# The prologue of an attention, rational and Sinkhorn-MoE kernel: load order, first two chunks of w_in, and the layout of q and k

## The chip, the cores and the metric

The kernel runs as one program on one core of a Trainium2 chip. The metric is the device time of one execution in microseconds (us). The core's engines are TensorE (PE in the profile, with its weight loads as PEld), VectorE (DVE), ScalarE (ACT), GpSimd (POOL) and SyncE (SP), which here only issues DMAs.

## The reference

Three layers follow each other; every layer feeds the next. The inputs q, k and v have 4 batches, 8 heads, 576 positions and 64 values a head; x then has 2304 rows of 512.

```python
scores = q @ k.T / sqrt(64)
mask_plain = (rel >= 0) & (rel < 32)                   # heads 0 to 3
mask_dil = (rel >= 0) & (rel < 128) & (rel % 4 == 0)   # heads 4 to 7
x = softmax(where(mask, scores, -1e9)) @ v             # to (2304, 512)

h = x @ w_in                                           # (512, 2048)
g = (a0 + a1*h + a2*h**2 + a3*h**3) / (1 + |b0|*|h| + |b1|*h**2 + 1e-6)
x = g @ w_out                                          # (2048, 512)

P = exp(x @ w_gate - max); 8 rounds of row and column scaling
out = sum over 8 experts of P[:, e] * (relu(x @ w1[e]) @ w2[e])
```

w_in and w_out arrive as 64-bit floats, and the kernel makes 32-bit floats of them itself.

## The kernel before

**Prologue.** The attention of batch 0 runs alone (`att_pieces(0)`, 52 pieces, then `flush`). Heads go in pairs (`pr` 0 and 1 are plain heads, 2 and 3 dilated ones), and each pair in three groups `jj` of 192 queries. A pair has four `prep` pieces (transposes of q and k on PE, evacuated to `qT` and `kT` by the ACTIVATE of L355), a group has a `qk` piece (scores, L363 and L370; maximum on DVE, L388; three Exp on ACT, L390; scaling on POOL, L396), a `tr` piece (transposes of the probabilities, L405, evacuated in L410) and an `av` piece (the product with v, L429, then a split into two float16 parts by L229 on ACT and L232 on DVE). The split needs a power of two for all of v's first half: `v_load` brings that half in three loads of 768 KB, `v_scan` takes its absolute maximum (L484), `v_scale` makes the scale (L207, L180, L194, L222 to L226). `coef0` (L557 to L560) prepares the rational function's coefficients from `abt`.

**Weights.** w_in is handled in four chunks of 512 columns. `wi_load(c)` issues four loads of 512 KB (L166). `wi_conv(c, kk)` turns a fourth of a chunk into float32 by `to_f32` (a Prelu on ACT, L492, and two operations on DVE, L496 and L497) and takes its maximum on ACT (L526). `wi_scale(c)` makes the chunk's scale and coefficients (L567). `wi_split(c, kk)` writes two float16 parts (L229 on ACT, L232 on DVE, 128x512). w_out is handled in sixteen blocks `f` by `wo_load` and `wo_split` (the same `to_f32`, then L607 on ACT and L611 on POOL).

**Rational stage.** 96 steps (six token blocks of 384 times sixteen blocks `f` of 128 columns) run as a pipeline: `rat_l1` (L634 to L636, twelve matmuls), the polynomials on ACT, DVE and POOL, and five steps later `rat_l2` (L694 to L696). Step `f` of the first block needs chunk `f // 4` of w_in, and block `f` of w_out five steps later. Each step has four slots in which other work is emitted: the attention of batches 1 to 3 (steps 0 to 14, 15 to 38, 43 to 62), the rest of w_in, w_out, and the maximum of v's second half. After it comes the MoE stage, almost all of the remaining time, with its own hand-placed slots.

**What sets the order.** The list of calls gives each instruction a place in an order of priority; a planner then simulates the program with costs of its own and orders each engine's instructions, so that a lower one can be taken ahead when the planner expects a higher one to wait. Attention pieces get a higher priority. What it has ordered is executed in order on each engine. `tc.add_manual_dep` adds a real wait of one instruction for another. `load` makes a DMA wait for the instruction in `gate_mm`: during the prologue the first matmul of the last emitted `qk`, later that of the last emitted `rat_l1`; while `gate_mm` is empty it waits for nothing. All loads are issued on SP's queue, in one order.

In the kernel before, the prologue's loads go out as: pair 0, v for two groups, pair 1, `abt`, v's first half, pair 2, v for six groups, pair 3. `extra` gives what is emitted after a piece of the prologue: `wi_load(0)` after piece 12, `wi_load(1)` after piece 30, `wi_conv(0, kk)` after 30, 32, 34 and 36, `wi_scale(0)` after 47, `wi_split(0, kk)` after 48 to 51. Chunk 1 is converted and split in slots of the rational stage's steps 0 to 3, though the planner took its conversion ahead.

For the plain heads, `att_load` puts positions 96c to 96c+95 into 96 partitions, for c = 0 to 5. A transposed third of a half is then a run of neighbouring positions:

```python
w, n = (QB, 6) if pr < 2 else (72, 8)
rows = [[D, w], [w * D, n], [1, D]] if pr < 2 else [[n * D, w], [D, n], [1, D]]
```

Of the kernel before, what the change touches and what calls it, by code (L numbers as in the profile page):

```python
# [10 lines left out]
F32 = mybir.dt.float32  # L11
# [16 lines left out]
def kernel(  # L28
# [14 lines left out]
    nc = tc.nc  # L43
# [152 lines left out]
    def across_sum(out_, in_, n):  # L196
        bt = side_matmul("smps", n, one.to_broadcast([P, P]), in_)
        nc.vector.tensor_scalar(out=out_, in0=bt[:, 0:n], scalar1=1e-9, scalar2=None, op0=ALU.add)

    def delayed(fn, k):  # L200
        return fn() if k == 0 else lambda: delayed(fn, k - 1)

# [64 lines left out]
    def att_load(b, pr, stage=None):  # L267
        off = (b * H + 2 * pr) * HSTR
        st = att.setdefault((b, pr), {})
        if stage:  # L270
            both = room(stage, [P, 2, 1024], F32)
        w, n = (QB, 6) if pr < 2 else (72, 8)
        rows = [[D, w], [w * D, n], [1, D]] if pr < 2 else [[n * D, w], [D, n], [1, D]]
        for i, (src, tag) in enumerate(((q, "aq"), (k, "ak"))):
            if stage:
                t = both[:w, i, 0:2 * n * D].rearrange("p (c h d) -> p h c d", c=n, h=2)
            else:
                t = room(tag, [w, n, 2, D], F32).rearrange("p c h d -> p h c d")
            for h in range(2):
                nc.sync.dma_start(out=t[:, h], in_=bass.AP(src.tensor, off + h * HSTR, rows))  # L280
            st[tag] = t.rearrange("p h c d -> p c (h d)")
# [49 lines left out]
    def att_prep(b, pr, x):  # L331
        st = att[b, pr]
        which, y = divmod(x, 2)
        key = "ak" if which else "aq"
        src = st[key]
        alt = b < 1 and pr % 2
        if x == 0:
            if ("qkT", alt) not in att:
                att["qkT", alt] = att_qk_tiles(alt)
            st["qT"], st["kT"] = att["qkT", alt]  # L340
        d = st["kT"][:, 32:] if which else st["qT"]
        if y == 1:
            st.pop(key)
        w, n = (QB, 3) if pr < 2 else (72, 4)
        bt = bank("qkps")
        for c in range(n):
            nc.tensor.transpose(bt[:, c * w:(c + 1) * w], src[:, n * y + c, :], ident[:w, :w])

        def after():
            if pr < 2:  # L350
                dv, ps = d[:, y * HS:(y + 1) * HS], bt[:, 0:HS]
            else:
                dv = d.rearrange("m (c p y) -> m y c p", c=4, y=2)[:, y]
                ps = bt[:, 0:HS].rearrange("m (c p) -> m c p", c=4)
            nc.scalar.activation(dv, ps, AF.Copy, scale=1.0 if which else QSCALE)  # L355

        return after

    def att_qk(b, pr, jj):
        st = att[b, pr]  # L360
        bt = bank("scps")
        i0 = MASK_AT[pr // 2, jj]
        mm = nc.tensor.matmul(bt[:, 0:3 * KW], ident_b, masks[:, i0:i0 + 3, :].rearrange("p a b -> p (a b)"), start=True, stop=False)  # L363
        if b == 0:
            gate_mm[0] = mm.ins
        for i in range(3):
            j = 3 * jj + i
            for h in range(2):
                hd = slice(h * D, (h + 1) * D)
                nc.tensor.matmul(  # L370
                    bt[hd, i * KW:(i + 1) * KW],
                    st["qT"][hd, j * 64:(j + 1) * 64],
                    st["kT"][hd, j * 64:j * 64 + KW],
                    start=False,
                    stop=i == 2,
                )
        sc = bt[:, 0:3 * KW].rearrange("q (i c) -> q i c", i=3)
        i = b * NG + pr * 3 + jj
        sx = sb.tile([P, 4, 3], F32, tag="asx", bufs=4, name="sx")
        y = i % (6 if b < 2 else 2)  # L380
        if y < 2:
            p = sb.tile([P, 3, KW], F32, tag=f"ap{y}", name="p")
        else:
            p = xpair[0][:, 3 * KW * (y - 2):3 * KW * (y - 1)].rearrange("p (a b) -> p a b", a=3)
        st["p", jj] = p

        def after():
            nc.vector.tensor_reduce(out=sx[:, 0, :], in_=sc, axis=AX, op=ALU.max, negate=True)  # L388
            for i in range(3):
                nc.scalar.activation(p[:, i, :], sc[:, i, :], AF.Exp, bias=sx[:, 0, i:i + 1], accum_out=sx[:, 1, i:i + 1])  # L390
            return norm

        def norm():
            nc.vector.tensor_scalar(out=sx[:, 2, :], in0=sx[:, 1, :], scalar1=1e-9, scalar2=None, op0=ALU.add)
            nc.vector.reciprocal(out=sx[:, 3, :], in_=sx[:, 2, :])
            nc.gpsimd.tensor_tensor(out=p, in0=p, in1=sx[:, 3, :].unsqueeze(2).to_broadcast([P, 3, KW]), op=ALU.mult)  # L396

        return after
# [81 lines left out]
    def v_scan(hf, i):  # L480
        t = vst.pop((hf, i))
        m = vmx[:, 6 * hf + 2 * i:6 * hf + 2 * i + 2]
        for j in range(2):
            nc.vector.tensor_reduce(out=m[:, j:j + 1], in_=t[:, j * NV // 2:(j + 1) * NV // 2], axis=AX, op=ALU.max, apply_absolute_value=True)  # L484

    def v_scale(hf):
        return pow2_scale(vmx[:, 6 * hf:6 * hf + 6], 6, 14, s_x1[:, hf:hf + 1], i_x1[:, hf:hf + 1], lag=hf)

    def to_f32(src, y, dst):
        w = src.rearrange("p (n two) -> p n two", two=2)  # L490
        lo, hi = w[:, :, 0], w[:, :, 1]
        nc.scalar.activation(y, hi.bitcast(F32), AF.Prelu, scale=float(2.0**-112), alpha=-float(2.0**32))  # L492
        d = y.bitcast(I32)

        def bits():
            nc.vector.tensor_scalar(out=d, in0=d, scalar1=3, scalar2=None, op0=ALU.logical_shift_left)  # L496
            nc.vector.scalar_tensor_tensor(out=dst.bitcast(I32), in0=lo, scalar=29, in1=d, op0=ALU.logical_shift_right, op1=ALU.bitwise_or)  # L497

        return bits
# [21 lines left out]
    def wi_conv(c, kk):  # L521
        x = wx[c][:, kk, :]
        i = c * KD + kk

        def mx():
            nc.scalar.activation(junk, x, AF.Abs, accum_out=wmx[:, i:i + 1])  # L526

        if not wide:
            junk = room(WI_ST[c][kk // 2], [P, 512], F32)
            return mx  # L530
        st = wst.pop((c, kk))
        junk = st[:, 0:512].bitcast(F32)
        bits = to_f32(st, x, x)

        def then():
            bits()
            return mx

        return then
# [50 lines left out]
    def wo_split(f):  # L590
# [4 lines left out]
        hi, lo = wo_hi[c][:, g, :], wo_lo[c][:, g, :]  # L595
        x, y = wst.pop(("o", f))
        if wide:
            bits = to_f32(x, y, y)
            x = y

        def s1():
# [10 lines left out]

        return s1


    behind = {}

    def pin(eng, i):
        if eng in behind:
            tc.add_manual_dep(i.ins, behind[eng], mybir.DependencyInfo(mybir.DependencyClass.Sync, mybir.DependencyReason.DATA), reason="behind work that others wait for")  # L620

    cur = {}
    SEQ = [(n, f, f == 0, f == NF1 - 1) for n in range(NB) for f in range(NF1)]
# [1 line left out]
    def rat_l1(st, half):  # L625
# [6 lines left out]
        for kk in (2 * half, 2 * half + 1):  # L632
# [3 lines left out]
            nc.tensor.matmul(hp, wlo, xb[:, 0, kk, :], start=False, stop=kk == KD - 1)  # L636
            if kk == 0:
                gate_mm[0] = mm.ins

    def cf(st):  # L640
        n, f, _, _ = SEQ[st]
# [494 lines left out]

    LAG = 5
    ATT = ((1, 0, 14), (2, 15, 38), (3, 43, 62))
    WO = [f if f < 8 else 11.75 + (f - 8) // 2 * 1.5 + 0.5 * (f % 2) for f in range(NF1)]
    WI_S = (None, 0, 4, 7.5)  # L1140

    def att_pieces(b):
        groups = [(pr, jj) for pr in range(H // 2) for jj in range(3)]
# [141 lines left out]
            if callable(more):  # L1285
                at(s + 1, more)

    for c in range(1, 4):
        s = int(4 * WI_S[c])
        for kk in range(KD):  # L1290
            at(s + 1 + 2 * kk, wi_conv, c, kk)
            at(s + (12 if c > 1 else 11) + kk, wi_split, c, kk)
        at(s + 10, wi_scale, c)
    for c in (2, 3):
        at(int(4 * WI_S[c]) - (6 if c == 2 else 4), wi_load, c)
    at(4 * 20, lambda: load(wgr, w_gate.rearrange("(k p) e -> p k e", p=P)))
    at(4 * 26 + 1, wg_prep)
    for i in range(3):
        at(4 * 1 + 8 * i, v_load, 1, i, "x2_4")
        at(4 * (1 + 2) + 8 * i, v_scan, 1, i)  # L1300
    at(4 * (1 + 8), v_scale, 1)
    at(4 * 13, coefs, 1, 0, 4)


    att_load(0, 0)
    for i in range(2):
        att_load_v(i)
    att_load(0, 1, "R1")
    nc.sync.dma_start(out=abt[:, 0:4], in_=ra.partition_broadcast(P))
    nc.sync.dma_start(out=abt[:, 4:6], in_=rb.partition_broadcast(P))  # L1310
    for i in range(3):
        v_load(0, i, f"x2_{3 + i}")
    att_load(0, 2, "R2")
    for i in range(2, 4):
        att_load_v(i)
    for i in range(4, 8):
        att_load_v(i)
    att_load(0, 3, "R3")
    pcs = att_pieces(0)
    extra = defaultdict(list)  # L1320
    extra[12].append(lambda: wi_load(0))
    extra[30].append(lambda: wi_load(1))
    av0 = next(i for i, pc in enumerate(pcs) if pc[0] == "av")
    extra[av0 - 1] += [lambda i=i: v_scan(0, i) for i in range(3)] + [lambda: v_scale(0), coef0]
    n = len(pcs)
    for kk in range(KD):
        extra[30 + 2 * kk].append(lambda kk=kk: wi_conv(0, kk))
        extra[n - 4 + kk].append(lambda kk=kk: wi_split(0, kk))
    extra[n - 4 - 1].append(lambda: wi_scale(0))
    for f in range(2):  # L1330
        extra[44 + f].append(lambda f=f: wo_load(f))
    later = []
# [89 lines left out]
```

## Time and profile before

| what | value |
|---|---|
| median of 3 runs | 1957.07 us (1953.51 to 1958.82) |
| time of the profiled execution | 1955.98 us |
| its span, first to last instruction | 1954.0 us |
| busy share of the span: PE, DVE, ACT, POOL | 96%, 79%, 62%, 25% |
| mean granted TensorE clock | 0.981 of full speed |

The profiled execution lies 1.1 us under the median, and 2.0 us of it lie outside the span. A row of instructions in the profile has a start, a length, the engine, the source line, the operation, output and inputs by name (`roomA`, `roomV` and `roomIG` are large shared buffers); a bracket at its end says how long the engine had been idle before it and what ended that. "SPq" rows are DMA issues in SP's queue.

### The profile page before, as it was taken

The numbers are of one execution on the slowest core, as the hardware profiler recorded it, in microseconds if no ns is written. First come the engines' busy times: TensorE is split into PE (matmuls) and PEld (weight loads), VectorE is DVE, ScalarE is ACT, GpSimd is POOL, SyncE is SP. The second block draws the span as 40 slices with busy tenths as digits, with TensorE's granted clock in tenths as the row PEclk, the third lists the DMA queues.
The fourth block names the chain that finished last, engine by engine and source line by source line (L and its number), as shares of the span: only waits on it lengthen the run. The fifth ranks groups of instructions, "written<-read, shape, count | busy, mean of one in ns | idle before, by whom it ended". The sixth has DMA issues, their size and how long they took to land. (4 is left out here: it accounts for less than half of the span.)

```text
span 1954.0 us, 36520 instructions
## 1 busy us (share of the span) xinstructions
PE 1875.1 (96%) x14202; PEld 1410.8 (72%) x14202; DVE 1543.8 (79%) x2516; ACT 1217.3 (62%) x2182; POOL 493.2 (25%) x489
## 2 busy tenths in 40 slices
PE   6688999999999899999999999999999999999998
PEld 5466777777776677777777777777777777777776
DVE  4799769678998999778688778877878787786754
ACT  5788777777776545647556655664656566465652
POOL 1233422222232023015113211411421231141110
PEclk6789999999999999999999999999999999999999
DMA  6744113122212351564454357345435534633323
GB/s 172 214 135 125 32 38 104 34 59 76 92 38 80 124 157 68 190 185 128 94 141 125 56 120 184 69 109 143 103 62 135 155 74 112 165 87 78 86 54 53
DMA packets 208269, 207.92 MB, mean 106 GB/s; under 512 B 78176, under 2 KB 155488, under 8 KB 208096
## 3 DMA queue, kind: packets, MB, share of 16 engines
q1 hardware_dynamic: 191232, 173.09, 29.4%
q0 software_dynamic: 16864, 32.51, 11.2%
q8 instruction: 111, 1.82, 0.4%
q14 instruction: 62, 0.51, 0.1%
HBM read 155.86 MB, written 49.68 MB: 105 GB/s over the span
## 5 line engine op out<-in xcount | busy, mean ns | idle before, releaser
L922 PEld LDWEIGHTS <-roomA 128*128 128x128 f16 x3276 | 318.9, 98 | 182.1 <-issue 14.2
L922 PE MATMUL l1a<-roomA 128*128 128x384 f16 x1872 | 355.8, 326 | 3.3 <-ACT roomV L971 2.5
L922 PE MATMUL l1b<-roomA 128*128 128x384 f16 x1404 | 273.6, 326 | 5.4 <-DVE roomA L973 3.4
L680 POOL TENSOR_TENSOR roomIG<-roomA,roomIG 128x384 fp32r<-128x384 f32 x96 | 118.2, 1242 | 230.6 <-ACT roomIG L679 206.0
L944 POOL TENSOR_TENSOR roomIG<-roomA 128x384 f32<-128x384 f32 x48 | 60.2, 1254 | 456.8 <-ACT roomA L978 344.3
L1022 PE MATMUL yps<-roomA 128*128 128x256 f16 x630 | 169.9, 273 | 2.4 <-DVE roomV L1048 1.5
L1022 PE MATMUL yps<-roomA,roomV 128*128 128x256 f16 x630 | 168.9, 273 | 3.1 <-DVE roomA L1045 3.1
L1023 PE MATMUL yps<-roomA,roomV 128*128 128x256 f16 x630 | 170.5, 273 | 0.8 <-DVE roomA L885 0.8
L1023 PE MATMUL yps<-roomA 128*128 128x256 f16 x630 | 170.9, 273 | 0.0
L1024 PE MATMUL yps<-roomA,roomV 128*128 128x256 f16 x630 | 169.4, 273 | 0.0
L1024 PE MATMUL yps<-roomA 128*128 128x256 f16 x630 | 169.1, 273 | 0.0
L871 POOL TENSOR_TENSOR roomA<-roomA 128x256 f32<-128x256 f32 x140 | 133.2, 971 | 35.0 <-DVE roomA L885 23.1
L695 PE MATMUL o1ps<-roomIG,roomV 128*128 128x384 f32 x384 | 137.0, 357 | 1.5 <-POOL roomIG L680 1.2
L885 DVE SCALAR_TENSOR_TENSOR roomA<-roomA,sm 128x768 f16<-128x768 f32 (+1 forms) x92 | 112.2, 1232 | 25.1 <-ACT roomA L882 24.3
L634 PE MATMUL h1ps<-roomA 128*128 128x384 f16 x384 | 128.5, 335 | 2.7 <-DVE roomA L660 1.3
L696 PE MATMUL o1ps<-roomIG,roomV 128*128 128x384 f32 x384 | 130.0, 341 | 0.0
L636 PE MATMUL h1ps<-roomA 128*128 128x384 f16 x384 | 127.9, 333 | 0.2 <-DVE roomA L232 0.2
L635 PE MATMUL h1ps<-roomA 128*128 128x384 f16 x384 | 128.0, 333 | 0.0
L944 POOL TENSOR_TENSOR roomIG<-roomV 128x384 f32<-128x384 f32 x48 | 51.1, 1064 | 288.7 <-ACT roomV L978 246.7
L1022 PEld LDWEIGHTS <-roomA 128*128 128x128 f16 x1008 | 98.4, 98 | 28.7 <-DVE roomA L1048 3.4
L1023 PEld LDWEIGHTS <-roomV 128*128 128x128 f16 x1008 | 98.4, 98 | 27.4 <-issue 4.2
L882 ACT ACTIVATE roomA<-roomA,sm 128x768 f16<-128x768 f32 (+1 forms) x92 | 93.9, 1036 | 38.9 <-POOL roomA L871 17.0
(221 smaller groups left out, 4925.5 us busy)
## 6 DMA issues: line engine op xcount, KB each, us to landing
roomA<-xd SPq DMA_DIRECT2D x119, 384.0 KB
roomA<-in_moe_w_dram SPq DMA_DIRECT2D x240, 128.0 KB
roomA<-in_moe_w_dram SPq DMA_DIRECT2D x120, 256.0 KB
out_dram<-roomV POOLq DMA_DIRECT2D x31, 512.0 KB, 5.7
out_dram<-roomA POOLq DMA_DIRECT2D x31, 512.0 KB, 5.8
roomV<-in_moe_w_in_dram SPq DMA_DIRECT2D x16, 512.0 KB
roomA<-in_moe_w_out_dram SPq DMA_DIRECT2D x16, 512.0 KB
xd<-roomA SPq DMA_DIRECT2D x14, 384.0 KB
```

The lines of the kernel that those rows point to most:

```text
L634: mm = nc.tensor.matmul(hp, whi, xb[:, 0, kk, :], start=kk == 0, stop=False)
L635: nc.tensor.matmul(hp, whi, xb[:, 1, kk, :], start=False, stop=False)
L636: nc.tensor.matmul(hp, wlo, xb[:, 0, kk, :], start=False, stop=kk == KD - 1)
L680: nc.gpsimd.tensor_tensor(out=gl, in0=g, in1=gh.bitcast(F32), op=ALU.subtract)
L695: nc.tensor.matmul(ob[dd], hi, d["gl"], start=False, stop=False)
L696: nc.tensor.matmul(ob[dd], lo, d["gh"], start=False, stop=last)
L871: pin("p" if pool else "v", eng.tensor_tensor(out=d[:, o, :], in0=a, in1=b, op=ALU.add if w == 0 and n == 0 else ALU.subtract))
L885: pin("v", nc.vector.scalar_tensor_tensor(out=l, in0=x, scalar=sc, in1=h, op0=ALU.mult, op1=ALU.subtract))
L922: mm = nc.tensor.matmul(ps, w[:, wx_, wh, kk * P:(kk + 1) * P], x[:, xh, kk, :], start=start and kk == 0 and wh == 0 and xh == 0, stop=sto ...
L1022: nc.tensor.matmul(o, hh[:, a - 1, c], w[:, m, 0, :], start=i == 0 and half == 0, stop=False)
L1023: nc.tensor.matmul(o, hh[:, a - 1, c], w[:, m, 1, :], start=False, stop=False)
L1024: nc.tensor.matmul(o, hl[:, a - 1, c], w[:, m, 0, :], start=False, stop=i == NP - 1 and (last or half == 1 or b == 3))
```

## The change

q and k of the plain heads are loaded with six neighbouring positions to a partition, as the dilated heads have eight; the evacuation in L355 then writes every sixth element of `qT` or `kT`. Pair 2 and v's scan are loaded ahead of `abt`, `wi_load(0)` is issued at the start, between `abt` and pair 3, and waits for nothing. `wi_load(1)` moves from piece 30 to 20. Both chunks are converted, scaled and split inside the prologue. A Prelu of `to_f32` now waits: for the last emitted Exp in chunks 0 and 1 ("x"), for the first matmul of the last emitted `rat_l1` in chunks 2 and 3 and in w_out ("m"); so do the maxima of v's second half. Chunk 2 moves two steps ahead (4 to 2), chunk 3 one and a half (7.5 to 6), the second half of v five steps later, and w_out's blocks 8 to 15 come once a step from step 10.25 (before: two in 1.5 steps from 11.75).

```diff
-        rows = [[D, w], [w * D, n], [1, D]] if pr < 2 else [[n * D, w], [D, n], [1, D]]
+        rows = [[n * D, w], [D, n], [1, D]]
...
             if pr < 2:
-                dv, ps = d[:, y * HS:(y + 1) * HS], bt[:, 0:HS]
+                dv = d.rearrange("m (p c) -> m c p", c=2 * n)[:, n * y:n * (y + 1)]
             else:
                 dv = d.rearrange("m (c p y) -> m y c p", c=4, y=2)[:, y]
-                ps = bt[:, 0:HS].rearrange("m (c p) -> m c p", c=4)
+            ps = bt[:, 0:HS].rearrange("m (c p) -> m c p", c=n)
...
-                nc.scalar.activation(p[:, i, :], sc[:, i, :], AF.Exp, bias=sx[:, 0, i:i + 1], accum_out=sx[:, 1, i:i + 1])
+                e = nc.scalar.activation(p[:, i, :], sc[:, i, :], AF.Exp, bias=sx[:, 0, i:i + 1], accum_out=sx[:, 1, i:i + 1])
+            behind["x"] = e.ins.name
...
+            r = nc.vector.tensor_reduce(out=m[:, j:j + 1], in_=t[:, j * NV // 2:(j + 1) * NV // 2], axis=AX, op=ALU.max, apply_absolute_value=True)
+            if hf:
+                pin("m", r)
...
-    def to_f32(src, y, dst):
+    def to_f32(src, y, dst, late):
...
-        nc.scalar.activation(y, hi.bitcast(F32), AF.Prelu, scale=float(2.0**-112), alpha=-float(2.0**32))
+        i = nc.scalar.activation(y, hi.bitcast(F32), AF.Prelu, scale=float(2.0**-112), alpha=-float(2.0**32))
+        pin(late, i)
...
-        bits = to_f32(st, x, x)
+        bits = to_f32(st, x, x, "x" if c < 2 else "m")
...
-            bits = to_f32(x, y, y)
+            bits = to_f32(x, y, y, "m")
...
                 gate_mm[0] = mm.ins
+                behind["m"] = mm.ins.name
...
-    WO = [f if f < 8 else 11.75 + (f - 8) // 2 * 1.5 + 0.5 * (f % 2) for f in range(NF1)]
-    WI_S = (None, 0, 4, 7.5)
+    WO = [f if f < 8 else f + 2.25 for f in range(NF1)]
+    WI_S = (None, None, 2, 6)
...
-        at(4 * 1 + 8 * i, v_load, 1, i, "x2_4")
-        at(4 * (1 + 2) + 8 * i, v_scan, 1, i)
-    at(4 * (1 + 8), v_scale, 1)
-    at(4 * 13, coefs, 1, 0, 4)
+        at(4 * 6 + 8 * i, v_load, 1, i, "x2_4")
+        at(4 * (6 + 2) + 8 * i, v_scan, 1, i)
+    at(4 * 13, v_scale, 1)
+    at(4 * 14 + 2, coefs, 1, 0, 4)
...
     att_load(0, 1, "R1")
+    att_load(0, 2, "R2")
+    for i in range(3):
+        v_load(0, i, f"x2_{3 + i}")
+    for i in range(2, 4):
+        att_load_v(i)
     nc.sync.dma_start(out=abt[:, 0:4], in_=ra.partition_broadcast(P))
     nc.sync.dma_start(out=abt[:, 4:6], in_=rb.partition_broadcast(P))
-    for i in range(3):
-        v_load(0, i, f"x2_{3 + i}")
-    att_load(0, 2, "R2")
-    for i in range(2, 4):
-        att_load_v(i)
+    wi_load(0)
+    att_load(0, 3, "R3")
     for i in range(4, 8):
         att_load_v(i)
-    att_load(0, 3, "R3")
...
-    extra[12].append(lambda: wi_load(0))
-    extra[30].append(lambda: wi_load(1))
+    extra[20].append(lambda: wi_load(1))
...
-    for kk in range(KD):
-        extra[30 + 2 * kk].append(lambda kk=kk: wi_conv(0, kk))
-        extra[n - 4 + kk].append(lambda kk=kk: wi_split(0, kk))
-    extra[n - 4 - 1].append(lambda: wi_scale(0))
+    for c, x in ((0, 26), (1, 36)):
+        for kk in range(KD):
+            extra[x + kk].append(lambda c=c, kk=kk: wi_conv(c, kk))
+            extra[x + 8 + kk].append(lambda c=c, kk=kk: wi_split(c, kk))
+        extra[x + 7].append(lambda c=c: wi_scale(c))
```

## Rows read from the trace of the kernel before

**Rows 1.** The page, part 1: busy us, share of the span, instructions of each engine.

```profile
PE 1875.1 (96%) x14202; PEld 1410.8 (72%) x14202; DVE 1543.8 (79%) x2516; ACT 1217.3 (62%) x2182; POOL 493.2 (25%) x489
```

**Rows 2.** Busy time by stretch: length, each engine (instructions), clock, DMA share, GB/s.

```profile
0.00:71.20 71.20, 45.15 (x397) 35.33 (x398) 36.85 (x113) 42.42 (x153) 11.40 (x33) 0.68 0.63 177
71.20:200.00 128.80, 110.18 (x819) 79.35 (x819) 117.84 (x244) 107.94 (x284) 48.07 (x45) 0.91 0.51 148
200.00:1954.00 1754.00, 1719.74 (x12990) 1296.16 (x12988) 1389.13 (x2160) 1066.98 (x1748) 433.71 (x413) 1.00 0.39 101
```

**Rows 3.** Waits of ACT, 0 to 71.2 us: us in total, times, longest.

```profile
ACT roomV L492 <- DMA roomV<-in_moe_w_in_dram: 11.9, 2, 7.3
```

**Rows 4.** Instructions in order of time, 34 to 72 us.

```profile
34.39 3.13 SPq L166 DMA_DIRECT2D roomV<-in_moe_w_in_dram  x4
36.83 1.19 PE L347 MATMUL qkps<-ident,roomA 72*128 72x72 f32 x8 [2.36 <-issue]
...
38.58 1.19 PE L347 MATMUL qkps<-ident,roomA 72*128 72x72 f32 x8 [0.55 <-DMA roomA<-in_k_dram]
...
40.64 0.66 ACT L492 ACTIVATE roomV<-roomV 128x512 f32<-128x512 f32 x1 [7.27 <-DMA roomV<-in_moe_w_in_dram]
...
43.23 0.84 PE L405 MATMUL ptps<-ident,roomA 128*96 128x128 f32 x3 [3.11 <-DVE roomA L232]
...
54.90 0.66 ACT L492 ACTIVATE roomV<-roomV 128x512 f32<-128x512 f32 x1 [4.63 <-DMA roomV<-in_moe_w_in_dram]
...
57.66 0.84 PE L405 MATMUL ptps<-ident,roomA 128*96 128x128 f32 x3 [5.65 <-DVE sx L395]
...
71.19 0.50 PE L634 MATMUL h1ps<-roomA 128*128 128x384 f16 x1
```

**Rows 5.** Busy time in two stretches of the prologue, columns as in rows 2.

```profile
16.00:20.00 4.00, 3.45 (x37) 2.85 (x36) 3.86 (x7) 1.54 (x5) 0.67 (x1) 0.50 1.01 326
...
25.00:71.20 46.20, 28.96 (x266) 21.92 (x266) 24.73 (x72) 30.70 (x105) 5.42 (x10) 0.61 0.61 172
```

**Rows 6.** ACT, 0 to 71.2 us, by line and shape: count, busy us, mean ns, idle before.

```profile
L492 ACT ACTIVATE roomV<-roomV 128x512 f32<-128x512 f32 x8 | 5.4, 674 | 11.9 <-DMA roomV<-in_moe_w_in_dram 11.9
L526 ACT ACTIVATE roomV<-roomV 128x512 f32<-128x512 f32 x8 | 5.3, 659 | 0.0
...
L355 ACT ACTIVATE roomA<-qkps 128x288 f32<-128x288 f32 x8 | 3.3, 420 | 3.8 <-PE qkps L347 3.6
...
L492 ACT ACTIVATE roomA<-roomA 128x512 f32<-128x512 f32 x2 | 1.5, 726 | 0.0
```

**Rows 7.** Instructions in order of time, 13 to 26 us.

```profile
14.24 0.21 DVE L559 TENSOR_SCALAR sm<-abt 128x1 int32<-128x1 int32 x2 [2.22 <-DMA abt<-in_moe_b_dram]
...
16.10 1.81 DVE L484 TENSOR_REDUCE sm<-roomA 128x1 f32<-128x768 f32 x2 [0.93 <-DMA roomA<-in_v_dram]
...
25.22 0.41 ACT L229 ACTIVATE roomA<-avps,sm 128x192 f16<-128x192 f32 x1
```

**Rows 8.** DMA packets from 1.5 to 4.6 us (pair 0) and 31.5 to 37 us (mostly pair 3).

```profile
DMA packets 2323, 0.58 MB, mean 187 GB/s; under 512 B 2323, under 2 KB 2323, under 8 KB 2323
...
DMA packets 2523, 0.70 MB, mean 127 GB/s; under 512 B 2508, under 2 KB 2508, under 8 KB 2522
```

**Rows 9.** Instructions of ACT, PE and DVE in order of time, 96 to 106 us.

```profile
96.28 0.96 PE L694 MATMUL o1ps<-roomIG,roomV 128*128 128x384 f32 x4 [3.69 <-ACT roomIG L679]
...
99.05 2.56 ACT L229 ACTIVATE roomA<-roomV,sm 128x512 f16<-128x512 f32 x4
...
103.71 2.06 DVE L232 SCALAR_TENSOR_TENSOR roomA<-roomV,sm,roomA 128x512 f16<-128x512 f32 x3
```

**Rows 10.** DVE, 71 to 200 us, by line and shape, columns as in rows 6.

```profile
L497 DVE SCALAR_TENSOR_TENSOR roomA<-roomA 128x512 int32<-128x512 int32 x14 | 10.9, 780 | 0.1
...
L232 DVE SCALAR_TENSOR_TENSOR roomA<-roomV,sm,roomA 128x512 f16<-128x512 f32 x12 | 8.4, 740 | 0.0
...
L496 DVE TENSOR_SCALAR roomA<-roomA 128x512 int32<-128x512 int32 x14 | 8.0, 569 | 0.8 <-ACT roomA L492 0.8
```

More of the change, by code (lines that the diff above doesn't have):

```diff
@@ L198, in across_sum, with pin @@
         nc.vector.tensor_scalar(out=out_, in0=bt[:, 0:n], scalar1=1e-9, scalar2=None, op0=ALU.add)
+    behind = {}
+    def pin(eng, i):
+        if eng in behind:
+            tc.add_manual_dep(i.ins, behind[eng], mybir.DependencyInfo(mybir.DependencyClass.Sync, mybir.DependencyReason.DATA), reason="behind work that others wait for")
     def delayed(fn, k):
@@ L483, in v_scan @@
         for j in range(2):
-            nc.vector.tensor_reduce(out=m[:, j:j + 1], in_=t[:, j * NV // 2:(j + 1) * NV // 2], axis=AX, op=ALU.max, apply_absolute_value=True)
+            r = nc.vector.tensor_reduce(out=m[:, j:j + 1], in_=t[:, j * NV // 2:(j + 1) * NV // 2], axis=AX, op=ALU.max, apply_absolute_value=True)
+            if hf:
+                pin("m", r)
     def v_scale(hf):
         return pow2_scale(vmx[:, 6 * hf:6 * hf + 6], 6, 14, s_x1[:, hf:hf + 1], i_x1[:, hf:hf + 1], lag=hf)
-    def to_f32(src, y, dst):
+    def to_f32(src, y, dst, late):
         w = src.rearrange("p (n two) -> p n two", two=2)
         lo, hi = w[:, :, 0], w[:, :, 1]
-        nc.scalar.activation(y, hi.bitcast(F32), AF.Prelu, scale=float(2.0**-112), alpha=-float(2.0**32))
+        i = nc.scalar.activation(y, hi.bitcast(F32), AF.Prelu, scale=float(2.0**-112), alpha=-float(2.0**32))
+        pin(late, i)
         d = y.bitcast(I32)
@@ L613, in wo_split @@
         return s1
[L616 to L620, printed above, removed]
     cur = {}
@@ L1286, in run_slot @@
                 at(s + 1, more)
-    for c in range(1, 4):
-        s = int(4 * WI_S[c])
+    for c in (2, 3):
+        s = 4 * WI_S[c]
+        at(s - 6, wi_load, c)
         for kk in range(KD):
             at(s + 1 + 2 * kk, wi_conv, c, kk)
-            at(s + (12 if c > 1 else 11) + kk, wi_split, c, kk)
+            at(s + 12 + kk, wi_split, c, kk)
         at(s + 10, wi_scale, c)
-    for c in (2, 3):
-        at(int(4 * WI_S[c]) - (6 if c == 2 else 4), wi_load, c)
     at(4 * 20, lambda: load(wgr, w_gate.rearrange("(k p) e -> p k e", p=P)))
```

## The prediction

> **What bounds the kernel now.** First the page's busy shares: PE leads with 96% of the span, DVE follows with 79% [rows 1]. An average over unlike stages says little about an edit near the start, so next the busy time by stretch. From 200 us on PE is busy 1719.7 of 1754 us; up to the first matmul of the rational stage, at 71.2 us, it is busy 45.2 us, at a granted clock of 0.68; in between 110 of 128.8 us, while DVE is busy 117.8 [rows 2]. So the kernel has three limits: a prologue in which nothing is full (ACT 42 of 71 us), a stretch in which the first steps of the rational stage share DVE with attention and weight work, and a long stage bound by PE. What the first two save is kept: they feed an engine that then has no idle time to lose or swallow.
>
> The change works on the first two. There I read the waits of ACT: 11.9 us in two waits of L492, the Prelu of w_in, for its DMA [rows 3]. The order of time shows what that does. Chunk 0 is issued at 34.39 us and its first Prelu starts at 40.64, after 7.27 us idle; the Exps of pair 3 stand behind it on ACT, so the next transposes on PE start only at 43.23, 3.11 us late. Before this PE waits 2.36 and 0.55 us for pair 3's q and k. At 54.90 the same happens with chunk 1: 4.63 us on ACT, 5.65 on PE. The first rational matmul comes at 71.19 [rows 4].
>
> **The prologue, step by step.** The four waits of PE are 2.36 + 0.55 + 3.11 + 5.65 = 11.7 us [rows 4], those of ACT 11.9 [rows 3]: two views of one loss, counted once. From 25 us on ACT is busy 30.7 of 46.2 us [rows 5], so it can become the limit itself; I make the sum on ACT. Taken away are the 11.9 us. Added are chunk 1's four splits, 2.56 us [rows 9], since its conversion is in the prologue already: L492 and L526 each count 8 there [rows 6]. Two Prelus of w_out, 2 x 0.726 = 1.5 us [rows 6], leave: their blocks are emitted in steps 0 and 1 and now wait for those steps' first matmuls. 46.2 - 11.9 + 2.6 - 1.5 = 35.4 us: the rational stage would start at 60.4 us, 10.8 earlier.
>
> Do the loads come in time? Everything goes through SP's queue in order. Ahead of the end of pair 3 now stand four pairs of 4 x 144 KB, v for four groups (0.6 MB), v's first half (2.4 MB) and chunk 0 (2.1 MB): 7.4 MB. Small packets move at 187 GB/s [rows 8], the big ones at 326 [rows 5]: 2.9 MB and 4.5 MB give 15.5 + 13.8 us, and with the start at 1.5 us pair 3 is there at 31, before PE asks for it (34.5 us before, and PE should be there a little earlier). Chunk 0 is there before it, at 28. The other bound is the prologue's mean of 177 GB/s [rows 2]: 42 us. I take 31, as the holes in that mean are mostly the times in which loads waited for matmuls. Chunk 1 comes behind the later groups of v, around 37 to 40 us, when its first Prelu (after piece 36) is due: between 0 and the 4.6 us of before, I take 0.8. v's first half is queued behind pair 2, 0.6 MB or 3 us; the scale it gives is used at 25.22 now [rows 7], and PE has pair 2's transposes to fill the gap with. `abt` now lands behind v, where DVE is waiting anyway; its wait of 2.22 us before [rows 7] may go or may turn into one for v (0.93 there now). Both at 0, with 3 us to either side.
>
> Neighbouring positions: each packet of the old plain pair 0 is under 512 B, and so are 2508 of 2523 while mostly the dilated pair 3, which has neighbours already, is moved [rows 8]. In the tile the two heads still alternate every 256 B. So I price the load at nothing; at most it saves pair 0 the difference between 187 and 326 GB/s, 0.58 MB or 1.3 us. PE's transposes are the same in number and size. A group's scores now need both halves of q and k, where the first group needed one: 0.4 us for one more L355 [rows 6] in each of two pairs. The masks' matmuls, which need neither, can run meanwhile, so I take nothing; without that cover it is 0.8 us.
>
> L355 writes every sixth element, 24 bytes apart. No row has such a stride: L492 reads every second word and takes 674 ns, L526 with all of them 659 [rows 6]. Lower bound nothing; upper bound a doubling, 0.42 us on each of 8 evacuations in the prologue, 3.4 us, and as much in batch 1. I take nothing, by the nearer row.
>
> The Trainium skill speaks against this edit: in "SBUF — State Buffer", section "Door 1: The DMA port swizzle (why [64,N] ≈ [32,N])", it says that SBUF has lines of 16 bytes and that every access that crosses to a new line pays. By it the sum would lose part or all of the upper bound. The row at 8 bytes agrees as far as it goes, and no run here shows 24.
>
> So the prologue gives 10.8 - 0.8 = **10 us**.
>
> **The stage from 71 to 200 us.** DVE sets the pace. It loses chunk 1's splits, 4 x 0.740 = 3.0 us, and gains the two w_out blocks, 2 x (0.569 + 0.780) = 2.7 us [rows 10]; almost nothing by load. But PE's wait of 3.69 us at 96 us [rows 9] falls where chunk 1's scale and splits crowd ACT and DVE, and those are gone; v's second half (6 maxima) moves from steps 3, 5 and 7 to 8, 10 and 12, which takes DVE work out of the crowded steps. Between 0 and 3.7, I take **2 us**. Earlier chunks 2 and 3 and the new spacing of w_out move work within the stage: nothing, as the total is the same.
>
> The pins: ACT executes in order, so a Prelu that waits for a step's first matmul holds the Exps, the evacuations and the polynomial's L657 queued behind it, and DVE and PE wait for these. That matmul needs only a free bank, and the planner knows the wait. I price it at nothing because ACT is idle for 21 of the stage's 129 us [rows 2]; without that cover it costs what the rival below says.
>
> **Sum.** 1956.0 (the profiled execution) - 10 - 2 = 1944; the median lies 1.1 above it: **1945 us**, 12 us or 0.6% faster. What a measurement here can tell from no change is about 0.3%, 5.9 us.
>
> **Rivals.**
> - *The queue only moves the waits.* Chunk 0 in front of pair 3 makes pair 3 land at 42 us, the bound at 177 GB/s. PE waits 8 us where I have none: 1945 + 8 = **1953**. For it: the whole prologue's rate is no better; against it: the full queue at 16 to 20 us moves 326 GB/s [rows 5]. It decides from a landing of about 37 us on. Chance 0.17.
> - *The pins stall ACT* (slower). 8 Prelus of chunks 2 and 3 and 16 of w_out wait, in a stage where PE runs late. If each costs the pace 1.2 us, 29 us are lost: 1945 + 29 = **1974**. It outweighs the gain from 0.5 us each, and makes the kernel measurably slower from 0.75. For it: a late PE would stop ACT, and ACT is what PE waits for; against it: DVE, not ACT, is full there. Chance 0.13.
> - *More is won.* PE's idle in the prologue is 26 us, 11.7 of them counted above; a third of the other 14 goes, as w_in's work fills ACT's holes before 40 us and PE's clock rises above 0.68; and PE's 18.6 idle us in the stage shrink by 5 more [rows 2]. 1945 - 10 = **1935**. Chance 0.20.
> - *The stride doubles L355,* with the page's rule as its mechanism: 3.4 us in the prologue and up to as much in batch 1, 1948 to 1952, middle **1950**. Chance 0.05, as the one strided row shows nothing.
>
> My forecast has the remaining 0.45. Faster by over 0.3% are the forecast, the larger gain and the stride: 0.70; the moved waits stay within: 0.17; the pins: 0.13. The range reaches from a little under the larger gain to just past the moved waits, 1932 to 1958; the pins stay outside, and so does a tail of the larger gain. The forecast's own range is 1940 to 1950.
>
> **What the profile would show.** Right: no long wait of L492 for w_in in the prologue; pair 3's transposes without a wait; L229 128x512 eight times before the first L634, which starts at 58 to 63 us; packets of the plain pairs still under 512 B; L355 at 0.42 us; DVE's busy time from there to 200 us about as now. Wrong: a wait of PE for q or k near 40 us; L492 waiting for L634 or DVE less busy in steps 0 to 15 than now; a first L634 at 60 us whose gain is gone by 200 us; or a planner that orders the MoE stage otherwise, which no row of before can show.

## The result, and the profile after

The changed kernel takes **1937.43 us** (median of 4 runs, 1933.23 to 1937.80) against 1957.59 for the kernel before: a ratio of 0.9896, 95% interval 0.9876 to 0.9916, or 20 us less. The forecast was 1945 with a range of 1932 to 1958, so sign and range held. But only 12 of the 20 us were forecast, the time lies outside the forecast's own range of 1940 to 1950, and the experiments show that the gain came from other places than the sum had put it. The profiled execution took 1937.8 us with a span of 1935.9, 18.1 less than before.

Line numbers have moved by 4 to 10: the evacuation of q and k is now L361, the Exps L396, transposes of the probabilities L412 with their evacuation L417, the `av` product L436, the splits L235 and L238, the Prelu L501, `rat_l1` L638 to L640 and the first operation of the polynomial L662 (before: L657). The same stretches as in [rows 2], of the changed kernel:

```profile
0.00:71.20 71.20, 45.72 (x429) 35.49 (x429) 41.68 (x127) 48.69 (x162) 12.29 (x34) 0.78 0.74 210
71.20:200.00 128.80, 114.08 (x861) 83.05 (x862) 120.92 (x247) 114.25 (x297) 54.96 (x51) 0.95 0.46 132
200.00:1935.90 1735.90, 1706.98 (x12915) 1286.58 (x12913) 1381.02 (x2144) 1058.27 (x1726) 429.25 (x405) 1.00 0.40 101
```

The first 200 us are fuller on every engine after the change: ACT is busy 163 us in place of 150, DVE 163 in place of 155. PE's granted clock is higher there too, 0.78 in place of 0.68 up to 71.2 us and 0.95 in place of 0.91 from there; what that is worth was not separated. The later stretch is shorter, but no less full. The waits of ACT up to 71.2 us, as in [rows 3]:

```profile
ACT roomA L396 <- DVE sx L394: 4.6, 2, 3.6
ACT roomA L361 <- PE qkps L353: 4.5, 3, 3.7
ACT roomV L501 <- DMA roomV<-in_moe_w_in_dram: 4.1, 2, 2.8
```

The 11.9 us for w_in have become 4.1. The instructions in order of time, as in [rows 4]:

```profile
18.75 1.81 DVE L491 TENSOR_REDUCE sm<-roomA 128x1 f32<-128x768 f32 x2 [2.51 <-DMA roomA<-in_v_dram]
...
22.09 0.47 PE L353 MATMUL qkps<-ident,roomA 72*128 72x72 f32 x4 [4.29 <-ACT roomA L396]
...
23.36 1.75 SPq L166 DMA_DIRECT2D roomV<-in_moe_w_in_dram  x4
...
34.27 1.28 PE L353 MATMUL qkps<-ident,roomA 72*128 72x72 f32 x16
...
35.20 1.22 ACT L501 ACTIVATE roomV<-roomV 128x512 f32<-128x512 f32 x2
...
42.73 1.87 SPq L166 DMA_DIRECT2D roomV<-in_moe_w_in_dram  x4
...
46.86 0.67 ACT L501 ACTIVATE roomV<-roomV 128x512 f32<-128x512 f32 x1 [2.78 <-DMA roomV<-in_moe_w_in_dram]
...
51.63 2.56 ACT L235 ACTIVATE roomA<-roomV,sm 128x512 f16<-128x512 f32 x4
...
55.57 1.82 PE L436 MATMUL avps<-roomA 96*64 96x64 f32 x24 [7.53 <-ACT roomA L417]
...
61.13 0.52 PE L638 MATMUL h1ps<-roomA 128*128 128x384 f16 x1
...
66.74 2.57 ACT L235 ACTIVATE roomA<-roomV,sm 128x512 f16<-128x512 f32 x4
...
72.83 0.34 ACT L396 ACTIVATE p<-scps,sx 128x96 f32<-128x96 f32 x1 [0.62 <-DVE sx L394]
...
73.79 0.67 ACT L662 ACTIVATE roomA<-h1ps,cf 128x384 f32<-128x384 f32 x1
```

Pair 3's transposes at 34.27 and chunk 0's first Prelus at 35.20 follow the instructions before them without idle time. Chunk 1 is issued at 42.73, later than thought, as v's loads stand before it in SP's queue, and the old wait is there in small. PE's longest wait, 7.53 us, is no longer for a load alone: between 49 and 55 us ACT converts chunk 1 and splits chunk 0 while PE waits for an evacuation. The first matmul of the rational stage comes at 61.13, as the sum said (60.4). But that marker misleads: after it the `av` products of batch 0 go on, ACT splits chunk 1 at 66.74 and takes batch 1's first Exps at 72.83, and the first polynomial starts at 73.79, only 1.4 us earlier than before (75.18). What was won by then is work done, not an earlier step. Busy time up to 76 us, of the kernel before and of the changed one:

```profile
0.00:76.00 76.00, 49.95 (x425) 38.70 (x426) 38.36 (x119) 45.62 (x162) 13.58 (x35) 0.69 0.61 171
```

```profile
0.00:76.00 76.00, 49.43 (x474) 37.89 (x475) 45.59 (x140) 52.88 (x179) 12.96 (x35) 0.80 0.74 205
```

DVE has 7.2 us more behind it and ACT 7.3 (a part of that because L361 is longer, below). So the kernels are compared at marks that every one has: the start of the 1st, 5th, 20th and 96th polynomial (96 instructions of L657 or its like, in order of time), and of the last of the 96 subtractions on POOL in the experts (L944 before). The last column is the time from the 20th polynomial to that, a stretch in which the edits change at most the layout of batches 2 and 3 and, in the two kernels called reordered, the place of w_gate's preparation by a step.

| kernel | median us | ratio, 95% interval | 1st | 5th | 20th | 96th | last expert | 20th to last |
|---|---|---|---|---|---|---|---|---|
| before | | | 75.18 | 108.05 | 213.12 | 585.06 | 1918.15 | 1705 |
| changed | 1937.4 | 0.9896 (0.9876-0.9916) | 73.79 | 98.03 | 200.09 | 570.61 | 1900.08 | 1700 |
| undo_layout | 1942.6 | 0.9937 (0.9923-0.9952) | 70.80 | 93.07 | 196.97 | 571.59 | 1904.69 | 1708 |
| layout_alone | 1953.5 | 0.9987 (0.9976-0.9998) | 73.40 | 106.98 | 210.81 | 580.28 | 1916.17 | 1705 |
| prologue_half | 1946.0 | 0.9945 (0.9929-0.9962) | 77.25 | 100.78 | 204.57 | 580.29 | 1908.79 | 1704 |
| stage_half | 1944.2 | 0.9945 (0.9930-0.9960) | 70.57 | 107.09 | 210.38 | 581.12 | 1910.07 | 1700 |
| stage_half_mended | 1953.3 | 0.9987 (0.9977-0.9997) | 72.06 | 100.18 | 205.47 | 581.39 | 1912.30 | 1707 |
| no_step_waits | 1954.6 | 0.9999 (0.9987-1.0011) | 86.46 | 108.40 | 214.70 | 586.58 | 1914.72 | 1700 |
| no_exp_waits | 1942.8 | 0.9939 (0.9921-0.9956) | 70.66 | 95.28 | 200.67 | 572.45 | 1906.81 | 1706 |
| chunk1_early | 1935.1 | 0.9899 (0.9882-0.9916) | 71.00 | 93.31 | 200.76 | 569.81 | 1897.41 | 1697 |
| chunk1_early_new_layout | 1942.8 | 0.9932 (0.9917-0.9947) | 74.06 | 98.28 | 204.05 | 578.55 | 1906.48 | 1702 |
| three_neighbours | 1953.1 (one run) | | 77.42 | 100.94 | 206.35 | 581.39 | 1915.61 | 1709 |
| control_reordered | 1946.5 | 0.9949 (0.9931-0.9968) | 74.46 | 108.50 | 214.41 | 581.26 | 1909.66 | 1695 |
| best_early_reordered | 1933.5 | 0.9893 (0.9874-0.9912) | 70.77 | 94.69 | 198.75 | 568.93 | 1895.80 | 1697 |

The ratio is to the kernel before on the same chip. 13.0 of the changed kernel's 18.1 us of span are there at the 20th polynomial; the other 5.0 appear after it.

Each mark is read from one traced execution. Two pairs of kernels show how far that carries: on ACT, DVE and POOL the kernel before and `control_reordered` have the same order of instructions up to 254 us, `undo_layout` and `best_early_reordered` up to 238 us, and yet their 1st polynomials differ by 0.7 and 0.0 us, their 5th by 0.5 and 1.6, their 20th by 1.3 and 1.8. Differences of marks as small as these say nothing.

### The profile page after: what moved, and what is told of

Read it like the earlier page. It is cut to its first block, busy times and chain, and to the rows that moved or that the text cites. A ratio compares the mean times of both kernels' runs of the same rounds, so it can differ in the third digit from the quotient of the medians.

```text
span 1935.9 us, 36515 instructions
## 1 busy us (share of the span) xinstructions
PE 1866.8 (96%) x14202; PEld 1405.1 (73%) x14202; DVE 1543.6 (80%) x2516; ACT 1221.2 (63%) x2182; POOL 496.5 (26%) x489
## 5 line engine op out<-in xcount | busy, mean ns | idle before, releaser
L638 PE MATMUL h1ps<-roomA 128*128 128x384 f16 x384 | 127.9, 334 | 7.0 <-ACT roomA L396 2.1
L640 PE MATMUL h1ps<-roomA 128*128 128x384 f16 x384 | 127.8, 333 | 0.0
L993 ACT ACTIVATE roomV<-roomIG 128x1536 f16<-128x1536 f32 x48 | 71.0, 1480 | 72.4 <-DVE roomIG L949 72.4
```

What stands on the lines that cost most here:

```text
L638: mm = nc.tensor.matmul(hp, whi, xb[:, 0, kk, :], start=kk == 0, stop=False)
```

## The experiments

**The layout undone** in the changed kernel.

```diff
-        rows = [[n * D, w], [D, n], [1, D]]
+        rows = [[D, w], [w * D, n], [1, D]] if pr < 2 else [[n * D, w], [D, n], [1, D]]
...
-                dv = d.rearrange("m (p c) -> m c p", c=2 * n)[:, n * y:n * (y + 1)]
+                dv, ps = d[:, y * HS:(y + 1) * HS], bt[:, 0:HS]
```

> The changed kernel with the old layout of q and k for plain heads. If the 24-byte stride is what makes L361 slow (0.58 to 0.75 us for the plain heads, 0.42 before), the evacuations are back at 0.42 to 0.44 us, some 0.28 us x 32 = 9 us of ACT less in all, 4.5 of them before 200 us where ACT and DVE set the pace, and the first transposes start at 4.4 us as before, not 5.0: 1932 to 1935 us. If the layout's neighbours help the loads: 1940 us or more. If nothing there is on the path: 1937.

ACT by line and shape: the changed kernel from 60 to 74 us (plain heads of batch 1 only), then the undone layout from 0 to 45 us (columns as in [rows 6]).

```profile
L361 ACT ACTIVATE roomA<-qkps 128x288 f32<-128x288 f32 x4 | 2.9, 722 | 0.5 <-PE qkps L353 0.5
```

```profile
L361 ACT ACTIVATE roomA<-qkps 128x288 f32<-128x288 f32 x8 | 3.4, 419 | 4.3 <-PE qkps L353 4.2
```

The evacuation is back at 419 ns, from some 700. The first and the twentieth polynomial start 3.0 and 3.1 us earlier: up to there the stride costs two thirds of the 4.5 us expected. And yet the end is 5 us later, where 2 to 5 earlier was expected, all of it after the twentieth step. The planner had ordered the later instructions otherwise, on ACT, DVE and POOL alike. Either the layout pays late, or reordering does; the next runs separate these.

**The layout alone**, put into the kernel before (the same lines, the other way).

> The kernel before with only the new layout of q and k for plain heads. If the 24-byte stride is all that the layout changes on the chip: L355 at 0.58 to 0.75 us for plain heads, the first polynomial 2 to 4 us later than before, 1959 to 1962 us at the end. If the neighbours help the loads, as the 5 us lost by undoing the layout suggest: 1950 to 1953. If those 5 us came from another order of the later instructions: anywhere within some 5 us of before, with the first steps still 2 to 4 us late.

0.13% faster, hardly to be told from nothing, where the first expectation had 1959 to 1962 us, and the first polynomial 1.8 us earlier, not later, with L355 as slow as in the changed kernel. By the second expectation 1950 to 1953 was the mark of faster loads; the time is just past its edge, but the stretch after the 20th polynomial is as long as before (1705 us). What makes the early steps 2 us earlier is open: the order has changed there too, and 2 us is little more than two executions of one order differ by. So the price of the stride does not show in this kernel.

**A control**: the kernel before with one unrelated call a step later.

```diff
-    at(4 * 26 + 1, wg_prep)
+    at(4 * 27 + 1, wg_prep)
```

> The kernel before with the preparation of w_gate emitted one step later (27, not 26): no work is added, removed or moved by more than a step, but the planner then orders much of what follows otherwise. It shows what reordering alone is worth: if the later differences between variants are such, this run may lie 2 to 5 us from before to either side; if not, it lies within 1 us.

8.6 us faster, more than the 2 to 5 us expected, with no work added or taken. Up to the 20th polynomial, where the order is still the same, it is 1.3 us behind the kernel before; then it takes 1695 us where that takes 1705. Busy time in this stretch, first of the kernel before, then of the control:

```profile
213.00:1918.00 1705.00, 1679.01 (x12658) 1260.96 (x12657) 1365.60 (x2117) 1049.20 (x1714) 420.71 (x401) 1.00 0.40 102
```

```profile
214.00:1910.00 1696.00, 1677.14 (x12655) 1260.69 (x12655) 1364.45 (x2117) 1049.98 (x1715) 426.15 (x402) 1.00 0.40 102
```

The same work, 26 us of idle PE in the one and 19 in the other. The order alone is worth more here than many edits, and edits that shift the early steps draw a new one: the fourteen kernels lie between 1695 and 1709 us, with PE busy for 1676 to 1684 of them. This can account for the 5 us that the undone layout lost late without any effect of the layout (the last run tests that), and it is why the halves below are compared at the 20th polynomial.

**The stage's half**: the kernel before with the waits for a step's first matmul and the stage's new slots. In its first form chunk 2 was loaded into a staging area from which chunk 1 was still to be read, so part of chunk 1's values are not its own; the work is the same in kind and amount.

```diff
+                behind["m"] = mm.ins.name
...
+        pin(late, i)
...
-    WO = [f if f < 8 else 11.75 + (f - 8) // 2 * 1.5 + 0.5 * (f % 2) for f in range(NF1)]
+    WO = [f if f < 8 else f + 2.25 for f in range(NF1)]
```

> The kernel before with only the rational stage's part of the change: the waits for a step's first matmul, the new slots of w_out, of chunks 2 and 3 and of v's second half; prologue, chunk 1 and layout as before. If the prologue brought the gain: 1954 to 1958 us. If the waits and slots brought most of it: 1943 to 1948. If the waits stall ACT: over 1963.

> The kernel before with only the waits for a step's first matmul, the new slots of w_out's blocks 8 to 15 and of v's second half; chunks 1 to 3 in their old slots (the earlier run loaded chunk 2 into a staging area that chunk 1 still used). If the waits and these slots bring some 10 us by themselves: 1944 to 1949 us, gained after the first polynomial. If the gain of the earlier run came from chunk 2's and 3's slots: 1953 to 1958.

The mended form, with chunks 1 to 3 in their old slots, has the 1st polynomial 3.1 and the 20th 7.7 us earlier. In the trace 5.9 of it is left at the last expert, 1707 us being one of the longer stretches; between the medians it is 1.7, as the traced execution was 2.7 us faster than its median. The first form's 11 us are 2.7 us at the 20th polynomial and a lucky order: its end says nothing on the edit.

**The prologue's half**: load order, both chunks in the prologue, waits for the Exps; old layout, old slots.

> The kernel before with only the prologue's part: the load order, w_in's first two chunks converted and split in the prologue behind the Exps; layout, slots and the other waits as before. If the prologue brought the gain: 1940 to 1945 us, with the first polynomial not much earlier than before (75 us) but the fifth some 10 us earlier. If the waits and slots did: 1952 to 1957.

8.6 us at the 20th polynomial, with the 1st 2.1 us *later* than before, and 1946.0 us at the end, a little above the 1940 to 1945 expected. At that mark the two halves seem to add up: 7.7 + 8.6 = 16.3, and the undone layout, which has both (and chunks 2 and 3 in new slots), stands at 16.1. But the mark does not need all the work that is due before it. These are the evacuations of the first token block's output, which end that block, in the kernel before, the changed one and `prologue_half`:

```profile
208.91 1.64 ACT L715 ACTIVATE roomA<-o1ps 128x384 f32<-128x384 f32 x4
```

```profile
195.29 1.64 ACT L720 ACTIVATE roomA<-o1ps 128x384 f32<-128x384 f32 x4
```

```profile
212.66 1.63 ACT L719 ACTIVATE roomA<-o1ps 128x384 f32<-128x384 f32 x4
```

In the first two they stand ahead of the 20th polynomial, in both halves behind it. The last of the four starts 13.6 us earlier than before in the changed kernel and 14.6 with the layout undone, but 3.1 us later in `stage_half_mended` and 3.7 later in `prologue_half`. Averaged over the polynomials from the 17th to the 32nd, `prologue_half` is 4.5 us ahead of the kernel before, `stage_half_mended` 5.9, the undone layout 15.7 and the changed kernel 12.5. So each half alone is worth some 4 to 6 us, and some 5 come only with both (chunks 2 and 3 in new slots, which neither half has, may be a part of that). What keeps the prologue's half down stands in its order on ACT:

```profile
59.86 0.66 ACT L501 ACTIVATE roomA<-roomA 128x512 f32<-128x512 f32 x1 [4.97 <-DMA roomA<-in_moe_w_out_dram]
```

A Prelu of w_out, taken ahead of batch 0's last splits, stands before its load; with the waits for a step's first matmul added, in the undone layout, the same wait is 0.77 us. The next run shows this from the other side.

**Without the waits for a step's first matmul** (slots as changed).

```diff
-                behind["m"] = mm.ins.name
```

> The changed kernel without the waits for a step's first matmul (Prelus of chunks 2 and 3 and of w_out, maxima of v's second half), slots as changed. The part with these waits and slots gave 7.7 us by the twentieth polynomial. If the waits keep late work from standing in front of the steps: the twentieth polynomial at 204 to 208 us (200.1 with them). If the slots did it alone: 199 to 201. The end may lie 5 us to either side of what follows from this, by reordering.

No time is left of the gain: the 1st polynomial comes 12.7 us later than with the waits, the 20th 14.6, far outside the 204 to 208 us expected; the end of the first token block comes 20.3 us later. The order of time on ACT shows how:

```profile
62.47 0.66 ACT L501 ACTIVATE roomA<-roomA 128x512 f32<-128x512 f32 x1 [6.35 <-DMA roomA<-in_moe_w_out_dram]
63.03 1.22 ACT L501 ACTIVATE roomV<-roomV 128x512 f32<-128x512 f32 x2
64.16 0.65 ACT L501 ACTIVATE roomA<-roomA 128x512 f32<-128x512 f32 x1
...
72.78 0.66 ACT L501 ACTIVATE roomV<-roomV 128x512 f32<-128x512 f32 x1 [1.09 <-DMA roomV<-in_moe_w_in_dram]
...
86.46 0.72 ACT L661 ACTIVATE roomA<-h1ps,cf 128x384 f32<-128x384 f32 x1
```

With earlier loads the planner takes w_out's first Prelu (`roomA`) ahead of chunk 1's last two (`roomV`, 63.03) and of batch 0's last splits, and chunk 2's four (`roomV`, from 72.78) ahead of the first polynomial. ACT, which runs in order, stands 6.35 us at w_out's DMA; most of the rest of the 12.7 us is the work on chunk 2, some 6 us of ACT. The old kind of wait is back, for another load.

**Without the waits for an Exp**, the others kept.

```diff
-            behind["x"] = e.ins.name
```

> The changed kernel without the waits of chunk 0's and 1's Prelus for an Exp. If these keep ACT from standing at w_in's DMA before the Exps: ACT waits longer for w_in in the prologue than 4.1 us, the first polynomial 2 to 5 us later, the twentieth at 202 to 205 us. If the earlier loads did it: the same 200 us, as w_in's chunk 0 is there when it is asked for.

ACT waits 7.9 us for w_in, not 4.1, yet the 1st polynomial is 3.1 us earlier and the 20th the same (200.67). Up to there these waits are worth nothing; the 5 us at the end come in the later stretch (1706 us).

**Chunk 1 early**, with the old layout and with the new one.

```diff
     att_load(0, 3, "R3")
+    wi_load(1)
...
-    extra[20].append(lambda: wi_load(1))
```

> The changed kernel with the old layout and the loads of w_in's chunk 1 issued directly behind pair 3, waiting for nothing (in the changed kernel they are issued at 42.7 us, and ACT waits 2.8 and 1.3 us for them, PE 7.5). If that wait is what is left of the old one: no wait of the Prelu for w_in in the prologue, 3 to 6 us faster than with the old layout alone. If ACT's work itself is the limit by then: the same as with the old layout alone.

> The changed kernel with the loads of chunk 1 issued directly behind pair 3, new layout kept; the order of instructions differs from the changed kernel's only in the first steps. If ACT's waits of 2.8 and 1.3 us for chunk 1 cost the path 4 us: 1932 to 1934 us. If ACT's work is the limit there: 1937.

With the old layout no wait of ACT for w_in is left in the prologue. The 1st polynomial does not move for that: 71.00 against 70.80 with the old layout, 74.06 against 73.79 with the new. But the wait is not simply gone: v's groups now come behind chunk 1, PE waits for v where it had not before (1.6 us at 41.9 us in the first, 1.2 at 24.0 and 1.3 at 43.2 in the second), and in the first ACT then waits 1.7 and 1.8 us for PE's products. Whether ACT's own work was the limit, or one wait took the other's place, these runs do not show. The 20th is 3.8 and 4.0 us later in the two pairs; why was not tried. The 7.5 us between the medians with the old layout are the later stretch, 1697 against 1708 us; with the new layout the median is 5.4 us later than the changed kernel's, where 0 to 5 earlier was expected.

**Three neighbours** to a partition, for the price of a stride: each head in two DMAs, positions 3p to 3p+2 of each half in partition p.

> The changed kernel with three neighbouring positions to a partition instead of six, so that L361 writes every third element (12 bytes apart); two DMAs a head in place of one. If lines of 16 bytes set the price, most writes go to a new line and L361 of plain heads takes 0.5 to 0.65 us; if any stride up to some 20 bytes is free, 0.42.

Single evacuations of plain heads, with three neighbours and with six (the changed kernel), and of a dilated head in the changed kernel, which writes 8 bytes apart:

```profile
5.48 0.56 ACT L365 ACTIVATE roomA<-qkps 128x288 f32<-128x288 f32 x1 [3.44 <-PE qkps L357]
```

```profile
63.70 0.71 ACT L361 ACTIVATE roomA<-qkps 128x288 f32<-128x288 f32 x1 [0.52 <-PE qkps L353]
```

```profile
28.02 0.42 ACT L361 ACTIVATE roomA<-qkps 128x288 f32<-128x288 f32 x1
```

0.42 us without a stride (the undone layout, above) and at 8 bytes, 0.56 at 12, 0.71 at 24, for the same 288 elements. The kernel's own time, of one execution and with twice the DMAs for plain heads, says nothing on the stride.

**The earliest start with another order**: the undone layout with w_gate's preparation a step later.

> The changed kernel with the old layout (the earliest of all at the twentieth polynomial, 197 us) and w_gate's preparation one step later, which reorders what follows. The stretch from the twentieth polynomial to the last expert block took 1695 to 1708 us in the runs so far: the end at 1930 to 1943 us, the twentieth polynomial at 197 us. If the 1708 us of the old layout belong to the layout and not to the order: 1941 to 1943.

1933.5 us, and the last stretch 1697 us: the 1708 of the undone layout were not the layout's. Its ratio, 0.9893, lies within the interval of the changed kernel's 0.9896, so it can't be called faster than that; it is the undone layout's order that it beats (0.9937, intervals apart).

## Why the prediction held, and where its sum was wrong

- *The loads come in time; the waits for them go.* Right for pair 3 and chunk 0, so the rival in which the queue moves the waits to pair 3 did not come. Half right for chunk 1, which was issued at 42.7 us behind v's loads; taking its wait away did not move the start. (The Exps at 41.20 us behind chunk 0's Prelu were pair 2's, not pair 3's, whose q and k were not yet evacuated; the sum does not depend on it.)
- *`abt` and v's first half at 0.* About right for DVE: no wait for `abt` is left, and one of 2.51 us for v stands in place of 2.22 and 0.93. But PE then waits 4.29 us for ACT at 22.09 us, behind that scan; what this cost was not tried.
- *The prologue gives 10 us, seen as a rational stage that starts 10.8 us earlier.* Too large for the prologue's half alone, 8.6 us at the 20th polynomial and 4.5 on the average of the 17th to 32nd, and the place was wrong. The time that the waits left went, by priority, to chunk 1's conversion and splits and to batch 1's attention; ACT is busy 32.3 of the 38.8 us from 35 us to the first polynomial. That the first matmul came at 61.13 for 60.4 was luck: the sum holds 2.6 us for chunk 1's four splits, which came only after it (66.74), and gives 57.8 without them. It was a bad mark besides, since PE fills its waits with it; the first polynomial hardly moved.
- *The stage gives 2 us, by chunk 1's crowd.* Mis-sized: its part alone measures 7.7 us at the 20th polynomial and 5.9 on that average. DVE's busy time was the wrong scale. In that stage it matters in which order the work comes, and `no_step_waits` shows that the waits do this.
- *The pins, priced at nothing, and 29 us lost if they stall ACT.* This is the step that failed most: the rival had the sign turned round. In the changed kernel 14.6 us of progress at the 20th polynomial hang on them. I had weighed the wait that they add, but not the waits at DMAs that they keep out: a Prelu that the planner takes early blocks an in-order engine until its load lands, 6.35 us without them. The prologue's earlier loads pay little without these waits (`prologue_half`).
- *The stride, priced at nothing with 3.4 us as the bound in the prologue.* The bound was nearer: 0.28 us more for each, 3.0 to 3.1 us at the 1st and 1.3 to 3.3 at the 20th polynomial, over the changed kernel and its two forms with the old layout and the pair with chunk 1 early. I had taken the row at 8 bytes for the nearest; it lies on the free side. The rule in the Trainium skill (its page "SBUF — State Buffer", section "Door 1: The DMA port swizzle (why `[64,N]` ≈ `[32,N]`)") is lines of 16 bytes, full speed with at least two accesses to a line and a price for each that crosses to a new one. It agrees with these runs: at 8 bytes apart the write is free, at 12 and 24 it costs 0.14 and 0.29 us for 288 elements.
- *Packets of the plain heads still under 512 B*: right, all 2507 from 1.5 to 5.5 us.
- *Another order of the MoE stage would make it wrong*: named, but no term and no width given to it. The last stretch differs by up to 14 us between the kernels here, and 5 of the 18.1 us between the two traces lie in it. Without them the forecast of 12 would have met 13.
- *More is won* (1935) came nearer than the forecast (1945), but not by its whole mechanism: PE's idle time up to 71.2 us did not shrink (25.5 us, 26.1 before), that from there to 200 us did by 3.9, and the clock rose.

So the number came out in part by luck. The sum added two terms that are not independent: each half alone gives some 4 to 6 us, and without the waits that were priced at nothing the whole change gives none (`no_step_waits`); the stride took back up to 3, and 5 us of the later stretch came on top.

## What to carry to other kernels

On an in-order engine ask of each load-dependent instruction what a planner may put behind it; a wait for something that comes just before its due time can be worth more than the earlier load. Where a planner orders the program anew after every edit, measure a control that changes the order and nothing else, and compare variants at marks close to the edit: here the control moved the end by 8.6 us and the whole change by 20. And take as a mark an instruction that needs all of the stage before it, not the first one that may slip in, and read more than one: at the 20th polynomial the halves seemed to add up, at the end of the first token block they did not.

## What the runs showed of the hardware

The price of a strided write on ACT was the surprise: 0.42, 0.56 and 0.71 us for 288 elements at 4, 12 and 24 bytes, and no more than 0.42 to 0.43 at 8 bytes, where the dilated heads write. And neighbours in DRAM made the load dearer to issue, and it moved no faster: 203 GB/s from 3 to 5 us, where the layout undone has 201, in packets under 512 B in both. The issues of pair 0 on SP, with the old layout and with six neighbours:

```profile
0.76 0.95 SPq L286 DMA_DIRECT2D roomA<-in_q_dram  x2
1.75 1.06 SPq L286 DMA_DIRECT2D roomA<-in_k_dram  x2
```

```profile
0.76 1.37 SPq L286 DMA_DIRECT2D roomA<-in_q_dram  x2
2.17 1.31 SPq L286 DMA_DIRECT2D roomA<-in_k_dram  x2
```

Four issues take 2.68 us in place of 2.01, and the first transposes start at 5.02 us in place of 4.63.
